# Scaling a pair behind the output copies, and transposing its q and k in two steps: one tuned attention-and-MoE kernel

## Chip, cores, metric

One core of one Trainium2 chip. The metric is the device time of one execution in microseconds, as the median of several runs. Spans quoted from profiles run from the first to the last instruction and are some 2 us shorter than the device time.

## The reference

Retention attention (batch 8, 8 heads, 576 positions, head size 64), then a feed-forward with Mish:

```python
scores = scale * np.matmul(q, k.transpose(0, 1, 3, 2))
gamma = 1.0 - 2.0 ** (-5.0 - np.arange(H))
Dmat = np.where(rel >= 0, gamma[:, None, None] ** rel[None, :, :], 0.0)
attn = np.matmul(scores * Dmat[None], v)
x = attn.transpose(0, 2, 1, 3).reshape(B * S, H * D)       # 4608 x 512
h = x @ w_in                                               # 512 -> 2048
out = (h * np.tanh(np.log1p(np.exp(h)))) @ w_out           # 2048 -> 512
```

## The kernel before

Rows are cut into 36 chunks of 128 positions; two chunks are a pair, four chunks a tile of the feed-forward. The decay is split into factors for q and for k, so VectorE scales both (`step_p`, into `qks`), TensorE transposes them (`step_t`, through an accumulator tile `sc`, copied to `qkT`), then come scores (`step_s`), state (`step_k`), output product (`step_o`, copied to `xT`). The feed-forward is `g1` (matmuls with w_in into `hp`, Mish on ScalarE into `gT`) and `g2` (matmuls with w_out into `ops` or `hp`, copied by VectorE to `res`). The order of the program is written by hand: attention steps stand between groups of feed-forward matmuls, so that their latencies pass beside them. An accumulator tile is the buffer that TensorE's matmuls write and that another engine copies out; `sc` and `hp` have two buffers each. From chunk 16 on the transposes are done by DMA.

```python
    def step_t(n):
        m, u = divmod(n, 2)
        ...
        tp = ps_sc.tile([P, 4, NP, P], BF16, name="sc")[:, 0:2]
        for i in range(2):                                  # q, then k
            flat = r["qks"][:, i, u].rearrange("p h d -> p (h d)")
            for p in range(NP):
                nc.tensor.transpose(tp[:, i, p, :], flat[:, ts(p, P)], ident)
        if n < 2 * NCH:
            nc.scalar.copy(r["qk"][:, 0, u], tp[:, 0])
            nc.vector.tensor_copy(r["qk"][:, 1, u], tp[:, 1])
        else:
            nc.scalar.copy(r["qk"][:, :, u], tp)
    ...
    def visit(m, w):              # pairs 4 to 7, beside eight groups w of matmuls
        n = 2 * m
        if w == 0:
            if 2 * m + 2 < NPE:
                load(m + 4)
        elif w == 2:
            if m == 5:
                step_k(1)
            one(n, "T")
        elif w == 3:
            one(n + 1, "T")
        elif w == 5:
            one(n, "S")
            one(n + 1, "S")
        elif w == 7:
            step_k(m)
            one(n, "O")
            one(n + 1, "O")
            if 2 * m + 2 < NPE:
                step_p(m + 1)
    ...                                     # chunk 3, before the first tile's g1
    first(3, "kQK")
    for f in range(4):
        g1_some(0, f, NCH - 1)
        first(3, {0: "S", 2: "O"}.get(f, ""))
    g1_chunk(3, 0)
```

## Time and profile before

| | value | where from |
|---|---|---|
| device time | 317.3 us (317.11 to 317.51) | 3 runs |
| span of the profiled run | 315.3 us | page |
| TensorE busy | 304.6 us, 97% | page, part 1 |
| VectorE, ScalarE busy | 134.9, 127.2 us | page, part 1 |
| TensorE's waits that the change could reach | 4.1 us | worked out in the prediction |

Read it so: TensorE is all but always at work, so a wait counts only where TensorE itself is held up. A wait is measured here from the start of one matmul to the start of the next, less the usual interval (216 ns for 512 columns, 56 ns for 128), and not by the idle figure in brackets.

### The profile page before, as it was taken

What the parts mean: (1) busy time and instruction counts of PE and PEld (TensorE: products, weight loads), DVE (VectorE), ACT (ScalarE), POOL (GpSimd) and SP (SyncE); (2) the same over time, 40 slices, a digit from 0 to 9 for tenths busy, and PEclk for the clock granted to TensorE, in tenths of its full rate; (3) what the DMA queues carried; (4) which work ended last, traced back from release to release, by engine and by line L of the source; (5) the groups of instructions that cost most, each with busy time, mean ns of one, the idle gap of its engine ahead of it and who ended that gap; (6) DMA issues with size and microseconds to landing.
All of it is one profiled execution on the core that took longest, in us unless ns stands there. A gap on an engine that the chain in (4) does not pass through costs nothing.

```text
span 315.3 us, 6082 instructions
## 1 busy us (share of the span) xinstructions
PE 304.6 (97%) x2635; PEld 158.8 (50%) x2635; DVE 134.9 (43%) x182; ACT 127.2 (40%) x212; POOL 78.7 (25%) x102
## 2 busy tenths in 40 slices
PE   6889999999999999999999999999999999999995
PEld 2455588655455554444545454445454545444444
DVE  5743574247738482626262626262626232001011
ACT  5667566324355542343434343434343432333300
POOL 6586672543340223122403040320000000000000
PEclk9999999999999999999999999999999999999999
DMA  6999999999996395969595969694040401000032
GB/s 171 261 178 223 197 208 221 201 228 246 221 238 79 78 199 113 189 102 197 131 174 116 185 127 175 139 163 103 33 102 33 102 33 35 33 33 35 33 83 83
DMA packets 72474, 43.38 MB, mean 138 GB/s; under 512 B 55680, under 2 KB 63616, under 8 KB 72448
## 3 DMA queue, kind: packets, MB, share of 16 engines
q0 software_dynamic: 43952, 26.22, 56.2%
q1 hardware_dynamic: 28352, 16.65, 21.3%
q8 instruction: 20, 0.33, 0.5%
q10 hardware_dynamic: 144, 0.13, 0.1%
q14 instruction: 6, 0.05, 0.0%
HBM read 36.70 MB, written 9.44 MB: 146 GB/s over the span
## 4 chain that ended last, share of the span: by engine, by line
PE 89%; DVE 3%; SPq 2%; DMA 2%; ACT 2%; issue 1%; DVEq 0%
PE hp L385 34%; PE ops L423 33%; PE hp L423 6%; PE hp L408 4%; PE sc L321 3%; PE sc L370 2%; PE sc L363 2%; SPq L137 2%; PE st L342 2%; DMA kraw<-in_k_dram 2%; PE sc L296 1%; PE hp L435 1%; DVE sm L324 1%; PE hp L396 1%; ACT qkT L298 0%
## 5 line engine op out<-in xcount | busy, mean ns | idle before, releaser
L385 PE MATMUL hp<-xT,w_in_t 128*128 128x512 bf16 x496 | 126.6, 380 | 0.7 <-ACT gT L387 0.7
L387 ACT ACTIVATE gT<-hp 128x512 bf16<-128x512 f32 x124 | 74.2, 599 | 128.5 <-PE hp L385 128.3
L423 PE MATMUL ops<-w_out_t,gT 128*128 128x512 bf16 x480 | 121.9, 379 | 0.2 <-DVE res L443 0.2
L423 PEld LDWEIGHTS <-gT 128*128 128x128 bf16 x560 | 54.2, 98 | 65.1 <-issue 1.3
L443 DVE COPY res<-ops 128x512 f32<-128x512 f32 x30 | 20.8, 692 | 129.0 <-PE ops L423 129.0
L385 PEld LDWEIGHTS <-w_in_t 128*128 128x128 bf16 x496 | 46.0, 98 | 53.8 <-issue 1.2
L324 DVE TENSOR_TENSOR sm<-sc,mask 128x1024 bf16<-128x1024 f32 x36 | 42.7, 1218 | 13.9 <-PE sc L321 13.9
L568 POOL COPY seen<-qkT 1x1 bf16<-1x1 bf16 x10 | 1.8, 178 | 128.2 <-DMA qkT<-qks 128.2
L346 ACT ACTIVATE ssb<-st,diag 128x512 bf16<-128x512 f32 x32 | 20.3, 685 | 15.5 <-PE st L342 15.5
L374 DVE CAST xT<-sc 128x512 bf16<-128x512 f32 x32 | 20.8, 686 | 6.7 <-PE sc L370 5.8
L107 POOL DMA_DIRECT2D qraw<-in_q_dram x16 | 17.2, 1074 | 13.1 <-DVE qks L280 7.5
L280 DVE TENSOR_TENSOR qks<-kraw,gk 128x1024 bf16<-128x1024 f32 (+1 forms) x18 | 19.8, 1102 | 0.0
L280 DVE TENSOR_TENSOR qks<-qraw,gq 128x1024 bf16<-128x1024 f32 (+1 forms) x18 | 19.8, 1098 | 0.0
L107 POOL DMA_DIRECT2D kraw<-in_k_dram x16 | 17.1, 1070 | 10.5 <-issue 4.9
L423 PE MATMUL hp<-w_out_t,gT 128*128 128x512 bf16 x80 | 18.8, 380 | 0.0
L107 POOL DMA_DIRECT2D v<-in_v_dram x16 | 17.2, 1074 | 6.2 <-DMA kraw<-in_k_dram 2.5
L408 PE MATMUL hp<-xT,w_in_t 128*128 128x128 bf16 x272 | 16.9, 219 | 0.0
L408 PEld LDWEIGHTS <-w_in_t 128*128 128x128 bf16 x272 | 15.4, 98 | 0.7 <-issue 0.2
L370 PE MATMUL sc<-sm,v 128*64 128x128 bf16 x288 | 13.8, 220 | 0.6 <-DVE sm L324 0.6
L321 PEld LDWEIGHTS <-qkT 64*128 64x128 bf16 x288 | 8.1, 94 | 9.8 <-issue 5.9
L410 ACT ACTIVATE gT<-hp 128x512 bf16<-128x512 f32 x17 | 10.2, 598 | 7.0 <-PE hp L408 6.8
L321 PE MATMUL sc<-qkT 64*128 64x128 bf16 x288 | 11.9, 218 | 1.1 <-DVE qkT L299 0.9
(75 smaller groups left out, 153.5 us busy)
## 6 DMA issues: line engine op xcount, KB each, us to landing
out_dram<-res SPq DMA_DIRECT2D x31, 256.0 KB, 3.5
qraw<-in_q_dram POOLq DMA_DIRECT2D x12, 512.0 KB, 8.1
kraw<-in_k_dram POOLq DMA_DIRECT2D x12, 512.0 KB, 9.3
v<-in_v_dram POOLq DMA_DIRECT2D x12, 256.0 KB, 9.8
qraw<-in_q_dram POOLq DMA_DIRECT2D x8, 256.0 KB, 9.4
kraw<-in_k_dram POOLq DMA_DIRECT2D x8, 256.0 KB, 9.4
w_out_t<-in_moe_w_out_dram POOLq DMA_DIRECT2D x4, 512.0 KB, 11.6
w_in_t<-in_moe_w_in_dram POOLq DMA_DIRECT2D x6, 256.0 KB, 7.1
```

The lines of the kernel that those rows point to most:

```text
L107: nc.gpsimd.dma_start(out=r[x][ds(off, ni)].rearrange("p u h d -> p (u h) d"), in_=src[ds(b, 2), :, ds(i0, ni), :].rearrange("b h p d -> p ...
L280: nc.vector.tensor_tensor(r["qks"][:, i, u], r["qk"[i]][:, u], g, op=OP.mult)
L321: nc.tensor.matmul(sc[:, e, p, :], lhsT=qk[r, 1, u, p, :], rhs=qk[r, 0, u, p, :], start=True, stop=True)
L324: nc.vector.tensor_tensor(sm.rearrange("p e n i -> p (e n) i"), sc.rearrange("p e n i -> p (e n) i"), (mask if len(chunks[n]) == 1 else ma ...
L346: nc.scalar.activation(ssb[:, :, :, e, :], st, AX.Copy, scale=diag[:, e:e + 1])
L370: nc.tensor.matmul(ot[ds(64 * e, 64), p, :], lhsT=vs[:, u, 2 * p + e, :], rhs=sm[:, e, p, :], start=(start and p == 0), stop=True, skip_gr ...
L374: (nc.scalar.copy if t == 0 else nc.vector.tensor_copy)(xts[t][:, :, ts(s, P)], ot)
L385: nc.tensor.matmul(hp, lhsT=w_in_t[:, c, ts(f, P)], rhs=xts[t][:, c, :], start=(c == 0), stop=(c == KC - 1))
L387: nc.scalar.activation(gts[t][:, f, :], hp, AX.Mish)
L408: nc.tensor.matmul(hp[:, j, :], lhsT=w_in_t[:, c, ts(f + j, P)], rhs=xts[t][:, c, ts(s, P)], start=(c == 0), stop=(c == KC - 1))
L423: nc.tensor.matmul(ops, lhsT=gts[t][:, f, ts(s, P)], rhs=w_out_t[:, f, :], start=(f == 0), stop=(f == nF - 1))
L443: copy(ot, ops)
```

## The change

The intent: a pair's scaling (two VectorE instructions of about 1.2 us) stood ahead of the copy of an output accumulator, and TensorE twice waited for the buffer. Scaling now follows that copy. It is then finished later, so transposes are regrouped: first q of both chunks of a pair, a group of feed-forward matmuls later k of both, into the same accumulator tile, from which ScalarE copies q in between. Chunks 4 to 7 also copy q as soon as it is transposed, ahead of k's transposes into the same tile; the first tile's steps are spread anew; the second tile's accumulators are copied by ScalarE instead of VectorE.

```diff
@@ -279,26 +279,43 @@
             g = (gq, gk)[i][:, place(2 * m), :].unsqueeze(1).unsqueeze(3).to_broadcast([P, nu, H, D])
             nc.vector.tensor_tensor(r["qks"][:, i, u], r["qk"[i]][:, u], g, op=OP.mult)
 
-    def step_t(n):
-
-        m, u = divmod(n, 2)
+    def turned(m):
         r = pairs[m]
         if "qk" not in r:
             r["qk"] = tr.tile([P, 2, 2, NP, P], BF16, name="qkT", bufs=3)
-        if n >= NPE:
-            nc.sync.dma_start_transpose(out=r["qk"].rearrange("p i u n t -> p (i u n) t"),
-                                        in_=r["qks"].rearrange("p i u h d -> p (i u h d)"))
-            return
-        tp = ps_sc.tile([P, 4, NP, P], BF16, name="sc")[:, 0:2]
-        for i in range(2):
+        return r["qk"]
+
+    def step_t(n):
+
+        m, u = divmod(n, 2)
+        qk = turned(m)
+        tp = ps_sc.tile([P, 4, NP, P], BF16, name="sc")
+        for i, copy in enumerate((nc.scalar.copy, nc.vector.tensor_copy)):
+            flat = pairs[m]["qks"][:, i, u].rearrange("p h d -> p (h d)")
+            for p in range(NP):
+                nc.tensor.transpose(tp[:, i, p, :], flat[:, ts(p, P)], ident)
+            copy(qk[:, i, u], tp[:, i])
+
+    def turn_pair(m, i):
+
+        r = pairs[m]
+        qk = turned(m)
+        if "tp" not in r:
+            r["tp"] = ps_sc.tile([P, 2, 2, NP, P], BF16, name="sc")
+        tp = r["tp"][:, i]
+        for u in range(2):
             flat = r["qks"][:, i, u].rearrange("p h d -> p (h d)")
             for p in range(NP):
-                nc.tensor.transpose(tp[:, i, p, :], flat[:, ts(p, P)], ident)
-        if n < 2 * NCH:
-            nc.scalar.copy(r["qk"][:, 0, u], tp[:, 0])
-            nc.vector.tensor_copy(r["qk"][:, 1, u], tp[:, 1])
-        else:
-            nc.scalar.copy(r["qk"][:, :, u], tp)
+                nc.tensor.transpose(tp[:, u, p, :], flat[:, ts(p, P)], ident)
+        nc.scalar.copy(qk[:, i], tp)
+
+    def cross(m):
+
+        r = pairs[m]
+        qk = turned(m)
+        nc.sync.dma_start_transpose(out=qk.rearrange("p i u n t -> p (i u n) t"),
+                                    in_=r["qks"].rearrange("p i u h d -> p (i u h d)"))
+        nc.gpsimd.tensor_copy(seen, qk[0:1, 0, 0, 0, 0:1])
 
     def step_n(m):
 
@@ -371,7 +388,7 @@
                                  start=(start and p == 0), stop=True, skip_group_check=True)
         if s == 0:
             xts[t] = xp.tile([P, KC, NCH * P], BF16, name="xT")
-        (nc.scalar.copy if t == 0 else nc.vector.tensor_copy)(xts[t][:, :, ts(s, P)], ot)
+        (nc.scalar.copy if t < 2 else nc.vector.tensor_copy)(xts[t][:, :, ts(s, P)], ot)
 
 
     gts = {}
@@ -501,23 +518,28 @@
     first(3, "V")
     keep_warm(3)
     first(2, "O")
-    first(3, "kQK")
-
-    for f in range(4):
+    first(3, "kQ")
+
+    steps = {0: "K", 1: "S", 3: "O"}
+    for f in range(5):
         g1_some(0, f, NCH - 1)
-        first(3, {0: "S", 2: "O"}.get(f, ""))
+        first(3, steps.get(f, ""))
     g1_chunk(3, 0)
-    for i in range(4, nF):
-        if i == 5:
+    g1_chunk(3, 4, 1)
+    for i in range(5, nF):
+        if i == 6:
             step_n(0)
-        elif i == 7:
+        elif i == 8:
             step_k(0)
         elif i == 9:
+            one(4, "P")
+        elif i == 10:
             step_n(1)
-        elif i == 12:
-            one(4, "PT")
+        elif i == 11:
+            one(4, "T")
+        elif i == 13:
+            one(4, "S")
         elif i == 14:
-            one(4, "S")
             one(5, "P")
         elif i == 15:
             one(4, "O")
@@ -544,14 +566,16 @@
 
         n = 2 * m
         if w == 0:
-            if 2 * m + 2 < NPE:
+            if m > 4:
+                step_p(m)
+            if n + 2 < NPE:
                 load(m + 4)
         elif w == 2:
             if m == 5:
                 step_k(1)
-            one(n, "T")
+            turn_pair(m, 0)
         elif w == 3:
-            one(n + 1, "T")
+            turn_pair(m, 1)
         elif w == 5:
             one(n, "S")
             one(n + 1, "S")
@@ -559,18 +583,11 @@
             step_k(m)
             one(n, "O")
             one(n + 1, "O")
-            if 2 * m + 2 < NPE:
-                step_p(m + 1)
-
-    def cross(m):
-
-        step_t(2 * m)
-        nc.gpsimd.tensor_copy(seen, pairs[m]["qk"][0:1, 0, 0, 0, 0:1])
 
 
 
     for i in range(nF):
-        if i == 6:
+        if i == 4:
             step_p(4)
         elif i >= 8:
             visit(4, i % 8)
@@ -580,9 +597,9 @@
         g2(1, i)
     for i in range(nF):
         visit(6 + i // 8, i % 8)
-        if i == 9:
+        if i == 10:
             step_p(8)
-        elif i == 11:
+        elif i == 12:
             cross(8)
             load(11)
         g1(2, i)
```

## The prediction

> **What bounds the kernel now.** I read the page first, then the waits of TensorE alone, then TensorE, ScalarE and VectorE in order of time from 17 to 130 us, where all the edited calls lie.
>
> From the page: engine totals, the chain's share by engine, and the two matmul groups of the MoE half.
> ```profile
> PE 304.6 (97%) x2635; PEld 158.8 (50%) x2635; DVE 134.9 (43%) x182; ACT 127.2 (40%) x212; POOL 78.7 (25%) x102
> ...
> PE 89%; DVE 3%; SPq 2%; DMA 2%; ACT 2%; issue 1%; DVEq 0%
> ...
> L385 PE MATMUL hp<-xT,w_in_t 128*128 128x512 bf16 x496 | 126.6, 380 | 0.7 <-ACT gT L387 0.7
> ...
> L423 PE MATMUL ops<-w_out_t,gT 128*128 128x512 bf16 x480 | 121.9, 379 | 0.2 <-DVE res L443 0.2
> ```
> TensorE is the bound; VectorE and ScalarE have more than half their time free. The 380 ns of one matmul is latency, not rate: four of them fill 0.86 us of the chain, 216 ns each. Nothing in the change removes matmul work, so only TensorE's waits can be won or lost. These are (us in total, times, longest):
> ```profile
> PE sc L321 <- DVE qkT L299: 0.9, 3, 0.3
> PE sc L262 <- ACT qkT L265: 0.8, 1, 0.8
> PE hp L385 <- ACT gT L387: 0.7, 1, 0.7
> ...
> PE sc L363 <- DVE sm L324: 0.3, 1, 0.3
> PE ops L423 <- DVE res L443: 0.2, 1, 0.2
> PE sc L321 <- DVE qkT L265: 0.2, 1, 0.2
> ```
> Each idle figure is short by the latency that the previous matmul's row still covers. From start to start, less the usual interval, the losses are 1.0 (at 18.24), 0.37 (19.48), 0.42 (35.49), 3 x 0.36 (38.73, 44.59, 50.08), 0.85 (86.61) and 0.41 us (101.16): 4.1 us, 1.3% of the time. That is the most the change can gain. From 130 us on it touches nothing.
>
> **What the Trainium skill says.** "Perfetto Trace Analysis", section "Identifying the Most-Contended Engine", calls matmul busy share a bad measure because matmuls are pipelined; the 380 against 216 ns agrees. "PSUM — Partial Sum Buffer", section "Engine vs sequencer instructions", has matmuls start in program order, so one that waits holds all behind it; no matmul in the trace passes one that waits. The same page, "PSUM bank collisions raise a hardware error", says accesses of two engines to one bank must be ordered by semaphores, reads against reads included. The trace agrees and shows more. In the four transposes of single chunks (first fence), VectorE's copy of k waits for ScalarE's copy of q though both only read (DVE qkT L299 waited for ACT qkT L298 four times, 5.6 us in all). In the second fence, k is transposed into the other bank of the same tile (2 KB further on), and still starts only when ScalarE's copy of q, 17.60 to 18.19, has ended:
> ```profile
> 31.51 0.61 PE L296 MATMUL sc<-ident,qks 128*128 128x128 bf16 x8
> 31.71 0.60 ACT L387 ACTIVATE gT<-hp 128x512 bf16<-128x512 f32 x1 [0.27 <-PE hp L385]
> ...
> 32.20 0.58 ACT L298 COPY qkT<-sc 128x512 bf16<-128x512 bf16 x1
> ...
> 32.81 0.43 DVE L299 COPY qkT<-sc 128x512 bf16<-128x512 bf16 x1 [1.80 <-ACT qkT L298]
> ```
> ```profile
> 17.02 0.40 PE L262 MATMUL sc<-ident,qks 128*128 128x128 bf16 x4
> 18.24 0.38 PE L262 MATMUL sc<-ident,qks 128*128 128x128 bf16 x4 [0.83 <-ACT qkT L265]
> ```
> So accesses to one accumulator tile by different engines are ordered as the program has them, across banks too. That decides this prediction: the new step_t and turn_pair emit q's copy before k's transposes, into the same tile. Before, all eight transposes stood ahead of any copy.
>
> **Part 1, chunk 3's transposes (17 to 24 us).** k now follows the first g1_some, which fills the 1.0 us gap. But that g1_some needs chunk 2's accumulators, whose copy on ScalarE ends at 17.71, so TensorE waits 0.5 us there (17.24 to 17.76). k's transposes come at 18.41; scores follow a k transpose by 1.24 us here (18.24 to 19.48), so they start at 19.65, after 0.26 us of waiting. Output product at 21.4 (scores plus 1.73, as before), next g1_some, then 0.18 us for chunk 3's copy; the 16-matmul g1_chunk from 22.57 to 23.47, the new 4-matmul one to 23.70. Then g1(0,5) needs one of two hp buffers: the g1_chunk's activation starts 0.2 us after its matmuls and takes 0.60, so TensorE waits till 24.31. Before, that work was done at 24.09 (start of the step_n transposes): +0.2 us.
>
> **Part 2, the rest of the first tile (24 to 37 us).** Scores and output product of chunk 4 move apart: -0.42. Chunk 4's transpose at x: the previous activation starts at x+0.20, q's copy at x+0.69 and ends at x+1.27 (first fence above: 31.51, 31.71, 32.20, 32.78). k's transposes can start 0.05 later, at x+1.32, while q's four (4 x 56 ns) are done at x+0.22: +1.10. Sum +0.7 us.
>
> **Part 3, chunks 5 to 7 (37 to 54 us).** The same 1.10 us three times. In exchange the wait of the scores for k's copy goes: from transposes to scores it was 1.79 us (36.94 to 38.73); now 0.22 + 1.10 + 0.22, 0.89 for sixteen matmuls and 0.1 of changeover make 2.53. +0.74 x 3 = +2.2 us. Accumulator copies moved from VectorE (686 ns) to ScalarE (590 ns) were on no wait of TensorE and stay so: 0.9 us or more lies between an output product and the matmuls that read its copy.
>
> **Part 4, pairs 4 to 7 (58 to 110 us).** Old transposes, each of q and k of one chunk, each with a tile of its own:
> ```profile
> 66.35 0.61 PE L296 MATMUL sc<-ident,qks 128*128 128x128 bf16 x8
> ...
> 67.05 1.01 ACT L301 COPY qkT<-sc 128x1024 bf16<-128x1024 bf16 x1 [8.54 <-PE sc L296]
> 67.66 0.61 PE L296 MATMUL sc<-ident,qks 128*128 128x128 bf16 x8
> ```
> The new ones have as many matmuls and copies of the same size, but share one tile. q's copy ends at x+1.71; k's transposes are reached at x+0.44+0.87 = x+1.31 and start at x+1.76: +0.45. In the second visit two ssb activations (1.27 us) stand before q's copy on ScalarE (76.76 to 78.03, copies from 77.91), so k starts at 78.95 instead of 77.97: +1.0. Third and fourth: +0.4 each (copies ending at 89.98 and 103.73 against transposes at 89.64 and 103.33). Sum +2.25.
> Against it, scaling now follows the output copies:
> ```profile
> 84.76 1.22 DVE L280 TENSOR_TENSOR qks<-qraw,gq 128x1024 bf16<-128x1024 f32 x1
> ...
> 86.61 1.02 PE L385 MATMUL hp<-xT,w_in_t 128*128 128x512 bf16 x4 [0.69 <-ACT gT L387]
> ...
> 87.03 0.69 DVE L443 COPY res<-hp 128x512 f32<-128x512 f32 x1
> ```
> The res copy is held up by two scalings and so keeps one of two hp buffers; the g1 at 86.61 must take the other, behind its activation. With the copy at 84.9 to 85.6 it starts at 85.76: -0.85. The copy at 100.42, behind another pair of scalings, goes to 99.2: -0.41. The scalings still end in time: q of pair 6 at about 86.7, used at 87.5; pair 8's at 104.5 with its DMA transpose landing 4.5 us later, used after 112. Sum of part 4: +1.0 us.
>
> **Total.** 0.2 + 0.7 + 2.2 + 1.0 = +4.1 us: 321.4 us.
>
> **Rivals.** (1) turn_pair's two halves lie in different banks and might go without a wait. For it: with no two engines in one bank no collision needs guarding. Against it: 18.24, where exactly that case waited. It would take 2.25 us off: 319.2. I give it one chance in ten, and take 0.2 off the total for it. (2) The author's intent holds and no transposes wait: the 4.1 us are won but for what part 1 keeps (about 1.6), so some 315. For it: only the fact that one makes such an edit to gain; against it, step_t's two halves share even a bank, where the trace shows the order kept. (3) Later scaling starves something: a raw buffer is freed 0.7 to 1 us later, so loads start later. Loads issued at 77 to 87 us land some 10 us on and are scaled after 115, so nothing comes of it; were a load to bind, up to 2 us more, 323. (4) ScalarE becomes a bound in chunks 5 to 7: per chunk it has four activations of 0.60, a q copy and an accumulator copy of 0.59 and sometimes 1.27 of ssb, 4.9 of over 5.5 us. In order and with little slack, it could lengthen q's copy by a further 0.5 us at two of the transposes: 322.4.
>
> **Range and chances.** 321.2 us. Rivals 1 and 4 set most of the range, 317.3 to 322.9; what lies below is rival 2. Within 2% means 311.0 to 323.6. Faster than that needs more than all waits gone: 0.01. Slower needs 2.3 us beyond my sum: 0.05. Same: 0.94.
>
> **What would show it.** TensorE's waits would list k's transposes on ScalarE's copy qkT: four times about 1 us as idle from chunks 4 to 7 and four times 0.3 to 0.9 from the pairs. "PE hp L385 <- ACT gT" at 86 and "PE ops <- DVE res" at 101 would be gone, with a new wait of 0.5 us on hp's activation near 24 us. VectorE's busy time falls by 4 x 0.69, ScalarE's rises by 4 x 0.59. If k's transposes start at the end of q's without that wait, the ordering I read at 18.24 isn't general, and the prediction is wrong by up to 6 us.

## The result

The changed kernel took 321.2 us (321.12 to 321.75, 4 runs), the kernel before 317.4 us (317.11 to 318.74, 4 runs). The ratio is 1.0115, 95% interval 1.0084 to 1.0146: slower clear of noise.

Line numbers shift in the changed kernel: transposes of chunks 4 to 7 are L296 and their copies L297, those of pairs L309 and L310, g1 is L402 (was L385), g2 is L440 (was L423), the scores L338 (was L321). Its waits of TensorE, all of them (us in total, times, longest):

```profile
PE sc L296 <- ACT qkT L297: 3.8, 4, 0.9
PE hp L262 <- DVE qks L247: 2.1, 3, 0.9
PE sc L309 <- ACT qkT L310: 1.7, 4, 0.8
PE ops L165 <- DVE line L185: 1.3, 1, 1.3
PE sc L387 <- DVE sm L341: 0.6, 2, 0.4
PE hp L402 <- ACT gT L427: 0.5, 1, 0.5
PE hp L413 <- ACT xT L391: 0.3, 1, 0.3
PE sc L338 <- DVE qkT L265: 0.2, 1, 0.2
```

The first and third rows are new: transposes wait for ScalarE's copy of qkT, eight times. The sixth and seventh (g1 on a buffer that a g1_chunk filled, and on chunk 2's copied accumulators) are new as well and belong to part 1 of the prediction. The waits of chunk 3's k transposes at 18 us, of the scores for k's copy (three), of the output product at 35 us, of g1 at 86 us and of g2 at 101 us are gone. Two rows of the first 16 us (L262 and L165) are the start-up and are there in both kernels, as are the 0.6 us on L387 (L370 before) and the 0.2 us on L338 (L321 before).

One of the first four, chunk 4, in order of time (start, length, engine, in brackets the idle time before it):

```profile
30.77 0.39 PE L296 MATMUL sc<-ident,qks 128*128 128x128 bf16 x4
30.97 0.60 ACT L404 ACTIVATE gT<-hp 128x512 bf16<-128x512 f32 x1 [0.71 <-PE hp L402]
...
31.46 0.58 ACT L297 COPY qkT<-sc 128x512 bf16<-128x512 bf16 x1
32.09 0.39 PE L296 MATMUL sc<-ident,qks 128*128 128x128 bf16 x4 [0.94 <-ACT qkT L297]
```

Before, these eight transposes stood in one row of x8 from 31.51. Now k's four start 1.32 us after q's, 0.05 us after q's copy ends. Without the wait they would start 0.22 us after.

The pairs, at the second visit, where two `ssb` activations (ScalarE's copies of the attention state) stand ahead of q's copy, and the place where g1 waited before, now clear:

```profile
80.13 0.62 PE L309 MATMUL sc<-ident,qks 128*128 128x128 bf16 x8
80.59 1.03 PE L440 MATMUL ops<-w_out_t,gT 128*128 128x512 bf16 x4
82.46 0.61 PE L309 MATMUL sc<-ident,qks 128*128 128x128 bf16 x8 [0.84 <-ACT qkT L310]
```
```profile
89.38 1.89 PE L402 MATMUL hp<-xT,w_in_t 128*128 128x512 bf16 x8
...
89.45 0.69 DVE L460 COPY res<-hp 128x512 f32<-128x512 f32 x1
90.06 1.21 DVE L280 TENSOR_TENSOR qks<-qraw,gq 128x1024 bf16<-128x1024 f32 x1
```

In the second fence, eight g1 matmuls in one row mean that the second group of four no longer waits: the res copy comes ahead of the scaling, as meant.

Where the time went, from the timelines of the two kernels (each stretch from one start on TensorE to the next):

| stretch | before | after | difference | predicted |
|---|---|---|---|---|
| q's transposes of chunk 3 to the same point of the first tile (as many g1 matmuls done) | 17.02 to 24.09 | 17.00 to 24.22 | +0.15 | +0.2 |
| to the transposes of chunk 5 | to 36.94 | to 37.74 | +0.67 | +0.7 |
| to the first g2 | to 57.71 | to 60.74 | +2.23 | +2.2 |
| to the scores of pair 8 | to 112.81 | to 116.94 | +1.10 | +1.0 |
| to the end of the span | to 315.3 | to 319.4 | 0.0 | 0 |

The differences add up to 4.1 us, which is the whole difference of the spans.

### The profile page after: what moved, and what is told of

It is laid out like the page before. It is cut to its first block, busy times and chain, and to the rows that moved or that the text cites. A ratio compares the mean times of both kernels' runs of the same rounds, so it can differ in the third digit from the quotient of the medians. Undisturbed runs are those within 1.5% of the kernel's fastest.

```text
span 319.4 us, 6100 instructions
## 1 busy us (share of the span) xinstructions
PE 305.4 (96%) x2639; PEld 159.4 (50%) x2639; DVE 132.6 (42%) x178; ACT 129.6 (41%) x217; POOL 79.1 (25%) x102
## 4 chain that ended last, share of the span: by engine, by line
PE 90%; ACT 3%; SPq 2%; DMA 2%; DVE 1%; issue 1%; ACTq 0%; DVEq 0%
PE hp L402 34%; PE ops L440 32%; PE hp L440 6%; PE hp L425 5%; PE sc L338 3%; PE sc L387 2%; PE sc L380 2%; SPq L137 2%; PE st L359 2%; DMA kraw<-in_k_dram 2%; ACT qkT L310 1%; PE sc L309 1%; PE hp L452 1%; PE hp L413 1%; ACT qkT L297 1%
## 5 line engine op out<-in xcount | busy, mean ns | idle before, releaser
L402 PE MATMUL hp<-xT,w_in_t 128*128 128x512 bf16 x492 | 125.6, 380 | 0.5 <-ACT gT L427 0.5
L404 ACT ACTIVATE gT<-hp 128x512 bf16<-128x512 f32 x123 | 73.4, 597 | 128.6 <-PE hp L402 128.3
L440 PE MATMUL ops<-w_out_t,gT 128*128 128x512 bf16 x480 | 121.9, 379 | 0.0
L440 PEld LDWEIGHTS <-gT 128*128 128x128 bf16 x560 | 54.2, 98 | 64.7 <-issue 0.8
L402 PEld LDWEIGHTS <-w_in_t 128*128 128x128 bf16 x492 | 45.6, 98 | 53.1 <-issue 0.8
L107 POOL DMA_DIRECT2D qraw<-in_q_dram x16 | 17.2, 1074 | 24.7 <-DVE qks L280 18.5
L391 DVE CAST xT<-sc 128x512 bf16<-128x512 f32 x28 | 18.0, 685 | 4.7 <-PE sc L387 3.9
L440 PE MATMUL hp<-w_out_t,gT 128*128 128x512 bf16 x80 | 18.8, 380 | 0.0
L387 PE MATMUL sc<-sm,v 128*64 128x128 bf16 x288 | 13.8, 220 | 0.6 <-DVE sm L341 0.6
L427 ACT ACTIVATE gT<-hp 128x512 bf16<-128x512 f32 (+1 forms) x18 | 10.3, 579 | 8.3 <-PE hp L425 8.1
L310 ACT COPY qkT<-sc 128x1024 bf16<-128x1024 bf16 x8 | 8.1, 1012 | 11.9 <-PE sc L309 11.9
L338 PEld LDWEIGHTS <-qkT 64*128 64x128 bf16 x288 | 8.1, 94 | 8.7 <-issue 6.4
```

The lines of the kernel that those rows point to most:

```text
L107: nc.gpsimd.dma_start(out=r[x][ds(off, ni)].rearrange("p u h d -> p (u h) d"), in_=src[ds(b, 2), :, ds(i0, ni), :].rearrange("b h p d -> p ...
L338: nc.tensor.matmul(sc[:, e, p, :], lhsT=qk[r, 1, u, p, :], rhs=qk[r, 0, u, p, :], start=True, stop=True)
L387: nc.tensor.matmul(ot[ds(64 * e, 64), p, :], lhsT=vs[:, u, 2 * p + e, :], rhs=sm[:, e, p, :], start=(start and p == 0), stop=True, skip_gr ...
L391: (nc.scalar.copy if t < 2 else nc.vector.tensor_copy)(xts[t][:, :, ts(s, P)], ot)
L402: nc.tensor.matmul(hp, lhsT=w_in_t[:, c, ts(f, P)], rhs=xts[t][:, c, :], start=(c == 0), stop=(c == KC - 1))
L404: nc.scalar.activation(gts[t][:, f, :], hp, AX.Mish)
```

## The experiments

Theory A is the prediction's: whatever moves, TensorE pays for q and k sharing one accumulator tile, because the second half's transposes are ordered behind the copy of the first. Theory B, the rival: the loss comes from the later scaling and the loads behind it, and the waits only show slack. In all eight runs below the results were correct. "Before" is 317.25 us (e1 to e4) and 317.14 us (e5 to e8), medians of seven runs each.

### e1: chunks 4 to 7 transposed as before

```diff
-        for i, copy in enumerate((nc.scalar.copy, nc.vector.tensor_copy)):
+        for i in range(2):
             ...                                   # four transposes
-            copy(qk[:, i, u], tp[:, i])
+        nc.scalar.copy(qk[:, 0, u], tp[:, 0])
+        nc.vector.tensor_copy(qk[:, 1, u], tp[:, 1])
```

> The changed kernel, with the transposes of chunks 4 to 7 as they were: all eight matmuls ahead of both copies. Theory A (TensorE waits for ScalarE's copy of q because k goes into the same tile): the four waits of 0.94 us on qkT go, three waits of 0.3 us of the scores for k's copy come back; 1.10 + 3 x 0.74 = 3.3 us less than the changed kernel, 317.9 us. Theory B (the loss comes from the later scaling and the later loads behind it, the waits only soak up slack): within 0.5 us of the changed kernel, 321.

Measured: 318.04 us (317.86 to 318.19), ratio to before 1.0024 (1.0007 to 1.0041). The four waits are gone, three shorter ones are back:

```profile
PE sc L339 <- DVE qkT L298: 0.9, 3, 0.3
```

Some 3.2 us of the changed kernel's time (321.2 less 318.04) belong to this one reordering. It cannot be late scaling: that was left as the change has it.

### e2: a tile of its own for q and for k of a pair

```diff
-        if "tp" not in r:
-            r["tp"] = ps_sc.tile([P, 2, 2, NP, P], BF16, name="sc")
-        tp = r["tp"][:, i]
+        tp = ps_sc.tile([P, 2, 2, NP, P], BF16, name="sc")[:, i]
```

> The changed kernel, with an accumulator tile of its own for q and for k of a pair; the two still lie in different banks, as they did. Theory A, ordering by tile: the four waits of pairs 4 to 7 (0.29, 0.84, 0.29, 0.29 us as idle; 0.46, 1.0, 0.46, 0.45 from start to start) go, 2.4 us less, 318.8 us. If the order were kept by something else than the tile (ScalarE's place in the program, the copies' target qkT), they stay: 321.2 us. Theory B: 321.

Measured: 318.77 us (318.64 to 318.85), ratio 1.0047 (1.0032 to 1.0062). TensorE waits no longer for a pair's copies; at the second visit k's transposes run while q's copy is only just beginning:

```profile
79.71 0.62 PE L307 MATMUL sc<-ident,qks 128*128 128x128 bf16 x8
...
80.97 1.92 ACT L308 COPY qkT<-sc 128x1024 bf16<-128x1024 bf16 x2
81.03 0.61 PE L307 MATMUL sc<-ident,qks 128*128 128x128 bf16 x8
```

The same matmuls, the same copies, the same place in the program; only the tile differs, and 2.4 us are gone.

### e3: own tiles for pairs and for chunks 4 to 7

```diff
-        tp = ps_sc.tile([P, 4, NP, P], BF16, name="sc")
         for i, copy in enumerate((nc.scalar.copy, nc.vector.tensor_copy)):
+            tp = ps_sc.tile([P, 4, NP, P], BF16, name="sc")[:, i]
             ...
-            copy(qk[:, i, u], tp[:, i])
+            copy(qk[:, i, u], tp)
```

(and the edit of e2.)

> The changed kernel, with own tiles for q and k both in pairs and in chunks 4 to 7. Theory A: 2.4 us of the pairs and 4 x 1.10 us of the chunks less, and the scores' waits for k's copy do not come back, as the two copies no longer wait for each other: 6.8 us less, 314.4 us, which is faster than the kernel before by 0.9%. Later scaling is all kept. Theory B: 320 to 321, as scaling and loads are as late as in the changed kernel.

Measured: 314.54 us (314.07 to 315.05), ratio 0.9915 (0.9900 to 0.9929): faster than the kernel before by 0.9%. All of the change's scaling is still in its late place, so theory B falls. In these chunks and pairs neither TensorE nor VectorE waits for ScalarE's copy of q; the two copies run side by side (chunk 4):

```profile
30.90 0.61 PE L296 MATMUL sc<-ident,qks 128*128 128x128 bf16 x8
...
31.55 0.42 DVE L297 COPY qkT<-sc 128x512 bf16<-128x512 bf16 x1 [0.62 <-PE sc L296]
31.59 0.58 ACT L297 COPY qkT<-sc 128x512 bf16<-128x512 bf16 x1
```

### e4: the kernel before, with only the scaling moved

```diff
         if w == 0:
+            if m > 4:
+                step_p(m)
...
-            if 2 * m + 2 < NPE:
-                step_p(m + 1)
```

(and `step_p(8)` and `cross(8)` one place later, as in the change.)

> The kernel before, with only the scaling of pairs 5 to 8 moved behind the output copies, the transposes still by chunk (q and k of one chunk together). The two waits at 86 and 101 us (0.85 and 0.41) go, but k of a chunk is now wanted before it is scaled: estimated 0.7, 0.15 and 0.3 us in pairs 5, 6 and 7. Theory A: 317.3 less 0.1, no gain to be seen, and waits of the transposes for scaling in the trace. Theory B: it already loses, 319 or more.

Measured: 317.43 us (316.82 to 317.89), ratio 1.0004 (0.9989 to 1.0019): no difference to be seen. The waits for hp and ops are gone, and these have come:

```profile
PE sc L296 <- DVE qks L280: 0.9, 2, 0.6
```

From start to start the waits cost 0.79, 0.27 and 0.40 us (pairs 5, 6 and 7; the second is short enough to lie under the previous row), against the estimated 0.7, 0.15 and 0.3: 1.46 us for the 1.26 us saved. So the reason for the two steps holds: late scaling gains nothing as long as k of the first chunk is wanted at once. e2 and e3 keep late scaling and the two steps, and there no transpose of a pair waits for scaling or for a copy; so it is the shared tile of the two steps that costs.

### e5: filling the wait for hp near 24 us

e3, with

```diff
-        if i == 6:
+        if i == 5:
             step_n(0)
```

> The kernel with own tiles for all halves (e3, 314.5 us), with the key transposes of step_n(0) one place earlier, between the short g1_chunk and g1(0,5). If the 0.46 us of TensorE before g1(0,5) is a wait for ScalarE to empty an hp buffer, the 0.45 us of transposes fill it: 314.1 us, and no wait of L400 on gT near 24 us. If that wait were for something that step_n itself delays, 314.5.

Measured: 314.11 us (313.99 to 314.19), ratio 0.9904 (0.9890 to 0.9919), 0.43 us less than e3. The two were measured in different calls and their intervals overlap, so it is the trace that decides: the wait of g1 on gT is no longer listed. It was a wait for one of two hp buffers, made by the change's short g1_chunk of four matmuls, after which TensorE reaches the next g1 only 0.2 us after the long g1_chunk's last matmul, before ScalarE has emptied either buffer.

### e6: the second tile's accumulators back on VectorE

```diff
-        (nc.scalar.copy if t < 2 else nc.vector.tensor_copy)(xts[t][:, :, ts(s, P)], ot)
+        (nc.scalar.copy if t == 0 else nc.vector.tensor_copy)(xts[t][:, :, ts(s, P)], ot)
```

> The changed kernel, with the second tile's accumulators copied by VectorE again. Theory A (on no wait of TensorE): 321.2 us, within 0.2. If the four copies on ScalarE push q's copies back there (rival 4 of the prediction), it is 0.5 to 2 us faster than the changed kernel.

Measured: 321.18 us (320.95 to 321.48), ratio 1.0128 (1.0113 to 1.0143), the changed kernel's time. Moving four copies between two engines that are half idle makes no difference to be seen, and the prediction's fourth rival, ScalarE as a bound, falls.

### e7: chunk 3 as before, its k in a tile of its own

e5, with `first(3, "kQK")` and the four `g1_some` and one `g1_chunk` of the kernel before, and this edit, whose else branch then takes an `sc` tile for q alone:

```diff
-        if n < NCH - 1:
+        if n < NCH - 1 or i:
             tp = ps_h.tile([P, 4, P], BF16, name="hp")
```

> e5 with chunk 3 as in the kernel before (k's transposes right behind q's, four g1_some, one g1_chunk), but k in a tile of its own out of the hp buffers. Theory A: k's transposes no longer wait, and scores come at about 18.5 us instead of 19.5; some 0.6 us less than e5, 313.5 us, 1.2% faster than the kernel before. If the first g1_some's wait for chunk 2's accumulators (17.7 us) takes all of it, 314.1.

Measured: 313.37 us (313.17 to 313.82), ratio 0.9883 (0.9869 to 0.9898), 1.2% faster than the kernel before and the fastest here (no execution of it overlaps e5's, but the intervals of the ratios overlap a little):

```profile
17.55 0.40 PE L260 MATMUL sc<-ident,qks 128*128 128x128 bf16 x4
17.81 0.40 PE L260 MATMUL hp<-ident,qks 128*128 128x128 bf16 x4
...
19.04 0.40 PE L334 MATMUL sc<-qkT 64*128 64x128 bf16 x8
```

k follows q after 0.26 us, where it took 1.22 us before, and the scores come 1.49 us after q's transposes instead of 2.46. This is the one wait of transposes for a copy out of their own tile that the kernel before already had, so the pattern gave a gain that the change had not aimed at. Against e5 two things differ, k's tile and the order of chunk 3's steps; from q's transposes to chunk 4's both together save 0.67 us (17.55 to 30.20 against 17.19 to 30.51), and no run takes them apart.

### e8: k in the other bank of the same tile

```diff
-                nc.tensor.transpose(tp[:, i, p, :], flat[:, ts(p, P)], ident)
-            copy(qk[:, i, u], tp[:, i])
+                nc.tensor.transpose(tp[:, 2 * i, p, :], flat[:, ts(p, P)], ident)
+            copy(qk[:, i, u], tp[:, 2 * i])
```

> The changed kernel, with k of chunks 4 to 7 in the other bank of the same tile (2 KB further on) instead of the same bank. If the order is kept for a whole tile, the four waits of 0.94 us stay: 321.2 us. If it is kept by bank, they go: 316.8 us.

Measured: 321.27 us (321.05 to 321.39), ratio 1.0132 (1.0115 to 1.0149), as the changed kernel. The four waits are the same to the last digit:

```profile
PE sc L296 <- ACT qkT L297: 3.8, 4, 0.9
```

With e3 this settles what the order hangs on: another bank does nothing, another tile takes the wait away. What keeps this order, the chip or the semaphores that the program was built with, no run here tests.

## Why the prediction was right, point by point

**The step it all rested on,** that accesses of two engines to one accumulator tile keep the program's order also across banks, was read from a single wait at 18.24 us. It holds: e8 shows it for chunks 4 to 7, e2 for pairs, e7 for the very place where it was read. Rival 1, to which one chance in ten was given, did not come about. That the 321.2 us were met to the last digit is luck: the bare sum was 321.4, and 0.2 us were taken off for that rival. What was right is the sum of the steps, 4.1 us, which the two spans show; the medians differ by 3.8, and the kernel before alone varied from 317.11 to 318.74 us.

**Part 1** came out at +0.15 instead of +0.2. The wait for chunk 2's accumulators is there (563 ns from start to start, 0.51 us lost; predicted 0.5), and so is the new wait for hp (0.46 us of idle time, from start to start 681 ns after a matmul of 128 columns where 56 is usual, so 0.62 lost, as predicted), and e5 shows what it was for.

**Parts 2 and 3** came out at +0.67 and +2.23. Each of the four waits costs 1156 to 1158 ns from start to start where 56 is usual: 1.10 us, the predicted figure. Its two components, a Mish activation ahead of the copy and the copy itself, lie in the timeline as they did before, and so could be read there.

**Part 4** came out at +1.10 instead of +1.0. The four waits of the pairs cost 0.46, 1.01, 0.46 and 0.45 us (intervals of 671, 1224, 671 and 670 ns less 216), 2.37 in all against the predicted 2.25; the savings at 86 and 101 us came in whole. Small as the miss is, it can be read: at the third visit ScalarE's copy began 0.70 us after the first transpose where the old timeline had 0.64; at the fourth it began at 0.70 in both, but the prediction counted only the 0.40 us until the copy's end and left out the 0.05 from there to the transposes, which it had counted at the first visit.

**What was said not to matter** does not: e6 for the accumulator copies, and the stretch after the scores of pair 8, which takes 202.5 us in both kernels. ScalarE's busy time rose by 2.4 us, as predicted; VectorE's fell by 2.3 where 2.8 was predicted. Rival 3, starved loads, has some colour, as GpSimd's issue of q loads waited 18.5 us for scalings instead of 7.5; but TensorE waits for no scaling of a pair in the changed kernel, and e3 is fast with the same late scaling.

**Rival 2,** the author's intent, did not come about in the changed kernel; e3 measures what it would have brought: with own tiles the edit gains 2.7 us (317.25 less 314.54), against the some 2.5 us that the prediction gave it (4.1 less 1.6).

## What to carry to other kernels

When work on one accumulator tile is cut in two steps so that something fits between them, ask what orders the second half behind the first: here a copy by another engine of the first half held up TensorE's writes to the second, although they shared no byte and, in the pairs and in e8, not even a bank. Give each half its own tile if the buffers allow it; two buffers were enough here and turned a loss of 1.2% into a gain of 0.9% (e3), and of 1.2% with e5's and e7's edits on top. And before moving work off the bound engine's path, add up that engine's waits first: 4.1 us was all there was to win, and eight new waits of 0.5 to 1.1 us, 6.8 us together, were enough to lose as much.

## What the Trainium skill lacked or had wrong

- "PSUM — Partial Sum Buffer", section "PSUM bank collisions raise a hardware error", gives bank and quadrant as what must be guarded. No page says that the order in a program like this one is kept for a whole accumulator tile, across banks: in e8 k lay in another bank and still waited four times, 1.10 us each, at 321.27 us.
- "Perfetto Trace Analysis", section "Matmuls" under "Optimizing Tensor Performance", advises rotating independent groups through different PSUM banks so that a copy passes beside the next matmuls. Here a different bank was not enough (e8, 321.27 us); a different tile was (e2, 318.77, and e3, 314.54 us).
- "TensorE: Matmul & The Clock Gate", section "Part 4: PE-mode transpose", gives a transpose of 128x128 by its duration, some 275 ns in a kernel; here the row of one is 219 ns long. What counted in all the sums here was the interval, which that section does not give: eight transposes take 0.44 us from the first start to the next matmul's (66.35 to 66.79 before), 56 ns each, at a granted clock of 1.0.
